# Top-k attention with two mixtures on one core: the first three weight requests of the first mixture placed behind the stores of conversion chunks 28, 30 and 31

## The chip, the cores and the metric

The kernel runs on 1 core of one Trainium2 chip. The metric is device time in microseconds, the median of several executions. TensorE is PE in the profile, VectorE DVE, ScalarE ACT, GpSimd POOL and SyncE SP.

## The reference, cut to what matters

```python
scores = q @ k.T / 8                      # 4 batches x 8 heads, 576 x 576, head size 64
scores = where(scores >= 32nd largest of the row, scores, -1e9)
x = softmax(scores) @ v                   # 2304 tokens x 512
h = x @ w_in                              # first mixture: 512 -> 2048
x = (max(h, 0) + alpha * min(h, 0)) @ w_out
# second mixture: tokens with x @ w_skip > 0 go to the best of 8 experts (512 -> 1024 -> 512)
out = x + gate * (relu(x @ w1[e]) @ w2[e])   # the other tokens keep x
```

## The kernel before, in words

Matrix products of the two mixtures are made exact enough by splitting each float32 operand into a rounded high part and the rest, and adding three products. For the first mixture the weights are split once, at the start, and the split copies are kept in device memory.

**Conversion.** `w_in` and `w_out` are cut into 32 chunks of 512 KB (`convs`). `conv_load` (lines 255 to 262) brings a raw chunk in through SP, into one half of a tile named `wr` (`cvtile`, lines 246 to 253). `convert` (lines 267 to 305) then makes three passes on ACT that read the raw chunk (lines 277, 279, 281), one on DVE (line 285), a rounding copy and a subtraction on POOL (lines 291 and 112), and a store through SP (lines 297 and 300) to `win` or `wout`. DVE's step, POOL's step and the store are put off by four slots each (`CV`, line 52), so a chunk passes through the engines while the next ones follow.

**Attention** runs in steps of 14 slots. Each slot issues what a hand-written table (`STEP`) puts there, for five units in different stages, and `slot` (line 1078) adds pieces of a list `todo` and whatever is due in the list `late`. The 32 conversions ride along in the first steps.

**The first mixture** of the first two blocks of rows starts when their attention columns are done (`queue_moe`, line 1175). Its pieces (`moe1`) multiply with `wr` tiles of 1 MB, read back from `win` and `wout` in a fixed order (`stream`). `fetch(j)` (line 569) asks for the j-th of them through POOL's queue (`wload`, line 549; the request itself is at line 551), if the chunks in it are converted and it wasn't asked for yet. There are three `wr` buffers, which conversion and mixture share: a request is held back until the buffer's last user is done. Later requests come from `need` (line 581), which asks for the weight in use, the next one and the one after that. The first three come from `store` of the last chunk:

```python
            if i == len(convs) - 1:
                late.extend((6 + j, lambda j=j: fetch(j)) for j in range(3))
```

They are issued six, seven and eight slots after chunk 31's store has been issued.

Every engine works through its own instructions in the order in which they were issued. What stands around the change is, on POOL: the last splits of `cv` tiles (chunks 29 to 31), the splits of the attention's output (`x` from `xf`, line 112) and the requests. On PE: transposes of the softmax (line 502), then the mixture's first products (`pm` from `x` and `wr`, line 604). On DVE: the attention's selection (lines 432 to 472), and the mixture's step `rn` (line 621), which needs ACT's `rn` (lines 614 and 615), which needs `pm`.

Of the kernel before, what the change touches and what calls it, by code (L numbers as in the profile page):

```python
# [62 lines left out]
def kernel(  # L63
# [46 lines left out]
    def sub(o, a, b):  # L110

        i = nc.gpsimd.tensor_tensor(o, a, b, op=OP.subtract)  # L112
        if gate[0] is not None:
            tc.add_manual_dep(i.ins, gate[0].ins.name, mybir.DependencyInfo(
                mybir.DependencyClass.Sync, mybir.DependencyReason.DATA), reason="the port is free then")
            gate[0] = None
# [120 lines left out]
    todo, late, convq, rowq = [], [], [], []  # L237
# [8 lines left out]
    def cvtile(i):  # L246

        if i:
            return moe.tile([128, 1024], F32, name="cv", tag="g", bufs=8)
        if not ring:  # L250
            t = moe.tile([128, 16, 128], F32R, name="wr", tag="wr", bufs=3).rearrange("p a c -> p (a c)").bitcast(F32)
            ring.extend(t[:, h * 1024:(h + 1) * 1024] for h in range(2))
        return ring.pop(0)

    def conv_load(kind, f):
        raw = cvtile(0).bitcast(I32).rearrange("p (d f t) -> p d f t", d=4, t=2)
        if kind == 0:
            nc.sync.dma_start(
                raw.rearrange("p d f t -> p d (f t)"),
                win32[:, f * 256:(f + 1) * 256].rearrange("(d p) f -> p d f", p=128))  # L260
        else:
            nc.sync.dma_start(raw.rearrange("p d f t -> p (d f t)"), wout32[f * 128:(f + 1) * 128, :])
        raws[kind, f] = raw

    convs = [(kd, f) for kd in range(2) for f in range(KF)]

    def convert(i):

        kind, f = convs[i]
        raw = raws.pop((kind, f))  # L270
        r2 = raw.rearrange("p d f t -> p (d f) t")
        hi, lo = r2[:, :, 1], r2[:, :, 0]
        hif = hi.bitcast(F32)
        w = cvtile(1).rearrange("p (a c) -> p a c", a=2)


        nc.scalar.activation(w[:, 0], hif, AF.Copy, scale=2.0 ** -112)
        t2 = w[:, 1].bitcast(U16).rearrange("p (c k) -> p c k", k=2)
        nc.scalar.activation(t2[:, :, 1].bitcast(mybir.dt.float16), hif, AF.Copy, scale=2.0 ** -60)
        top = raw.rearrange("p d f t -> p (d f t)").bitcast(U16).rearrange("p (c k) -> p c k", k=4)[:, :, 1]  # L280
        nc.scalar.activation(t2[:, :, 0], top, AF.Copy, scale=2.0 ** -13, bias=2.0 ** -14 - 0.5)

        def bits():
            t = w[:, 1].bitcast(I32)
            nc.vector.scalar_tensor_tensor(t, w[:, 0].bitcast(I32), 3, t, op0=OP.logical_shift_left,
                                           op1=OP.bitwise_or)
            if i + AHEAD < len(convs):
                conv_load(*convs[i + AHEAD])

        def split():  # L290
            nc.gpsimd.tensor_copy(w[:, 0].bitcast(F32R), w[:, 1])
            sub(w[:, 1].bitcast(F32R), w[:, 1], w[:, 0])

        def store():
            converted.add(i)
            if kind == 0:
                nc.sync.dma_start(win_s[f // 2][:, f % 2], w)
            else:
                for a in range(2):
                    nc.sync.dma_start(wout_s[f // 8][:, :, f % 8, a, :].rearrange("d p c -> p d c"),  # L300
                                      w[:, a].rearrange("p (d c) -> p d c", d=KD))
            if i == len(convs) - 1:
                late.extend((6 + j, lambda j=j: fetch(j)) for j in range(3))

        return none * (CV - 1) + [bits] + none * (CV - 1) + [split] + none * CV + [store]

# [242 lines left out]
    def wload(src):  # L549
        t = moe.tile([128, 16, 128], F32R, name="wr", tag="wr", bufs=3)  # L550
        nc.gpsimd.dma_start(t, src)
        return t
# [16 lines left out]
    def fetch(j):  # L569
        if j < len(stream) and j not in wr and stream[j][1] in converted:  # L570
            wr[j] = wload(stream[j][0])
# [904 lines left out]
```

## Time and profile before

| | us |
|---|---|
| median of 3 runs | 1110.81 (1108.39 to 1111.5) |
| the profiled execution | 1104.66 |
| its span, first to last instruction | 1102.9 |
| PE busy | 971.4 (88%) |
| DVE busy | 930.8 (84%) |
| ACT busy | 737.9 (67%) |
| POOL busy | 526.4 (48%) |

The span lies 1.8 us below the profiled execution's own time, and that execution is 6.2 us below the median of the runs. The conversion fills the first 145 us of the span. Busy shares are averages over stages; the rows further down come from the stretch of 30 us in which conversion ends and the mixture begins.

### The profile page before, as it was taken

What the parts mean: (1) busy time and instruction counts of PE and PEld (TensorE: products, weight loads), DVE (VectorE), ACT (ScalarE), POOL (GpSimd) and SP (SyncE); (2) the same over time, 40 slices, a digit from 0 to 9 for tenths busy, and PEclk for the clock granted to TensorE, in tenths of its full rate; (3) what the DMA queues carried; (4) which work ended last, traced back from release to release, by engine and by line L of the source; (5) the groups of instructions that cost most, each with busy time, mean ns of one, the idle gap of its engine ahead of it and who ended that gap; (6) DMA issues with size and microseconds to landing.
All of it is one profiled execution on the core that took longest, in us unless ns stands there. A gap on an engine that the chain in (4) does not pass through costs nothing.

```text
span 1102.9 us, 22357 instructions
## 1 busy us (share of the span) xinstructions
PE 971.4 (88%) x7270; PEld 854.3 (77%) x7270; DVE 930.8 (84%) x2943; ACT 737.9 (67%) x1932; POOL 526.4 (48%) x860
## 2 busy tenths in 40 slices
PE   4566469999999999899999999999999889898994
PEld 2444358888999888899888988998789778687883
DVE  6999969999998999899979989998993323798971
ACT  7978858667865785687568666856772433596860
POOL 5877746434653553366346425733552441326220
PEclk9997769999999999999989999999999998899997
DMA  8979876665675667656566676674556985799950
GB/s 246 323 233 291 252 227 203 222 217 175 214 229 179 206 209 245 205 196 218 192 196 197 215 239 218 200 227 165 181 192 241 368 308 206 276 362 397 344 197 8
DMA packets 154286, 254.17 MB, mean 230 GB/s; under 512 B 78062, under 2 KB 110830, under 8 KB 137776
## 3 DMA queue, kind: packets, MB, share of 16 engines
q0 software_dynamic: 20928, 138.73, 36.3%
q1 hardware_dynamic: 132032, 113.62, 32.9%
q8 instruction: 60, 0.98, 0.4%
q14 instruction: 66, 0.54, 0.1%
q10 hardware_dynamic: 1200, 0.30, 0.1%
HBM read 224.20 MB, written 29.71 MB: 230 GB/s over the span
## 4 chain that ended last, share of the span: by engine, by line
PE 49%; DVE 30%; DMA 8%; ACT 5%; issue 4%; POOL 3%; SPq 1%; POOLq 0%; DVEq 0%; ACTq 0%
PE pm L653 15%; PE pm L604 10%; DVE v L441 5%; DVE F L432 4%; PE px L536 4%; DVE Ex L472 4%; DVE m L432 4%; PE ps L411 4%; PE px L1029 4%; DVE F L444 4%; PE pm L1011 4%; PE pt L502 3%; DVE rn L621 3%; DMA wr<-wout 2%; DMA wr<-win 2%
## 5 line engine op out<-in xcount | busy, mean ns | idle before, releaser
L604 PE MATMUL pm<-x,wr 128*128 128x256 f32 (+1 forms) x1536 | 250.9, 311 | 16.7 <-DMA wr<-win 13.9
L653 PE MATMUL pm<-g,wr 128*128 128x256 f32 (+1 forms) x1536 | 241.4, 305 | 5.7 <-DMA wr<-wout 5.7
L604 PEld LDWEIGHTS pm<-x,wr 128*128 128x128 f32 x1536 | 217.5, 195 | 26.2 <-DMA wr<-win 9.0
L653 PEld LDWEIGHTS pm<-g,wr 128*128 128x128 f32 x1536 | 211.2, 190 | 14.4 <-issue 7.1
L441 DVE MAX8 v<-F 128x8 f32<-128x72 f32 (+2 forms) x576 | 213.1, 405 | 1.0
L416 ACT ACTIVATE sb<-ps 128x288 f32<-128x288 f32 x288 | 105.1, 413 | 95.2 <-PE ps L411 61.8
L112 POOL TENSOR_TENSOR g<-rn,g 128x256 fp32r<-128x256 f32 (+1 forms) x128 | 110.7, 874 | 71.2 <-ACT g L635 27.9
L411 PE MATMUL ps<-kT,qT 64*128 64x288 f32 x768 | 102.8, 357 | 28.5 <-ACT sb L416 15.8
L444 DVE MATCH_REPLACE8 F<-v,F 128x72 f32<-128x72 f32 (+1 forms) x432 | 122.9, 290 | 0.0
L472 DVE SCALAR_TENSOR_TENSOR Ex<-sb,v,Ex 128x577 f32<-128x577 f32 x144 | 121.3, 870 | 0.0
L411 PEld LDWEIGHTS ps<-kT,qT 64*128 64x128 f32 x768 | 66.7, 206 | 56.7 <-ACT sb L416 20.0
L621 DVE SCALAR_TENSOR_TENSOR rn<-rn,nalpha 128x256 f32<-128x256 f32 (+1 forms) x128 | 78.8, 616 | 36.4 <-ACT rn L615 34.8
L464 ACT ACTIVATE Ex<-sb,st 128x576 f32<-128x576 f32 x144 | 105.2, 780 | 0.3
L112 POOL TENSOR_TENSOR x<-xf,x 128x128 fp32r<-128x128 f32 (+1 forms) x80 | 41.3, 516 | 127.0 <-ACT x L545 121.5
L502 PE MATMUL pt<-ident,Ex 128*128 128x128 f32 x576 | 90.8, 294 | 0.0
L536 PE MATMUL px<-PT,vt 128*64 128x128 f32 (+1 forms) x1280 | 88.5, 285 | 0.0
L514 ACT ACTIVATE PT<-pt 128x512 f32<-128x512 f32 x144 | 86.4, 601 | 2.9 <-PE pt L502 2.7
L614 ACT ACTIVATE rn<-pm 128x256 f32<-128x256 f32 (+1 forms) x128 | 52.7, 412 | 52.0 <-PE pm L604 49.7
L502 PEld LDWEIGHTS pt<-ident,Ex 128*128 128x128 f32 x576 | 69.5, 149 | 10.9 <-issue 7.5
L536 PEld LDWEIGHTS px<-PT,vt 128*64 128x64 f32 x1280 | 69.5, 146 | 9.7 <-issue 1.8
L432 DVE TENSOR_TENSOR F<-m 128x144 f32<-128x144 f32 (+2 forms) x240 | 71.2, 348 | 0.0
L635 ACT ACTIVATE g<-rn 128x256 fp32r<-128x256 f32 (+1 forms) x128 | 56.4, 448 | 20.2 <-DVE rn L621 20.1
(431 smaller groups left out, 1908.8 us busy)
## 6 DMA issues: line engine op xcount, KB each, us to landing
wr<-win POOLq DMA_DIRECT2D x64, 1024.0 KB, 5.3
wr<-wout POOLq DMA_DIRECT2D x64, 1024.0 KB, 5.2
wraw<-in_moe_w_dram SPq DMA_DIRECT2D x88, 512.0 KB, 6.0
wr<-in_moe_w_in_dram SPq DMA_DIRECT2D x16, 512.0 KB, 5.4
vt<-in_v_dram SPq DMA_DIRECT2D x32, 256.0 KB, 4.0
win<-cv SPq DMA_DIRECT2D x16, 512.0 KB, 4.6
wr<-in_moe_w_out_dram SPq DMA_DIRECT2D x16, 512.0 KB, 5.0
wout<-cv SPq DMA_DIRECT2D x32, 256.0 KB, 3.3
```

The lines of the kernel that those rows point to most:

```text
L112: i = nc.gpsimd.tensor_tensor(o, a, b, op=OP.subtract)
L411: nc.tensor.matmul(self.ps[h, j][:, 0:HALF], lhsT=hd["q"][gp, a, u * 128:(u + 1) * 128], rhs=hd["k"][gp, b_, c0:c0 + HALF], **se)
L432: gate[0] = nc.vector.tensor_tensor(o[:, n_], a[:, n_, 0:w], a[:, n_, w:2 * w], op=op)
L441: nc.vector.max(v8[:, h, r, :], F[:, h, 0:w])
L444: nc.vector.match_replace(out=F[:, h, 0:w], in_to_replace=v8[:, h, r, :], in_values=F[:, h, 0:w], imm_value=NEG)
L464: nc.scalar.activation(self.Ex[:, h, :], self.sb[:, h, :], AF.Exp, bias=self.st[:, 0, h:h + 1], scale=0.125)
L472: nc.vector.scalar_tensor_tensor(self.Exp[:, cs], self.sbp[:, cs], v8[:, h, 3, 7:8], self.Exp[:, cs], op0=OP.is_ge, op1=OP.mult, accum_out ...
L502: nc.tensor.transpose(pt[:, c * 128:(c + 1) * 128], P[:, c0:c0 + 128], ident)
L536: nc.tensor.matmul(x[h * 64:(h + 1) * 64, 0:n], lhsT=hd["vt"][:, h, c, :], rhs=rhs, start=False, stop=(c == SF - 1))
L604: nc.tensor.matmul(hp[:, 0:n], lhsT=w[:, (f % 2) * 8 + a * 4 + d, :], rhs=x[:, d, c0:c1], start=(i == 0), stop=(i == 3 * KD - 1))
L621: nc.vector.scalar_tensor_tensor(rn[:, 0, 0:n], rn[:, 1, 0:n], nalpha[:, f:f + 1], rn[:, 0, 0:n], op0=OP.mult, op1=OP.add)
L653: nc.tensor.matmul(op_[:, 0:n], lhsT=w[:, 2 * f + a, :], rhs=g[(hf + ch) * 8 + f, sg][:, gg, 0:n], start=(i == 0), stop=(i == ni - 1))
```

## The change

The three requests leave the list of pieces that are put off, and are issued at once: the first right behind the store of chunk 28, the second behind that of chunk 30, the third behind that of chunk 31.

```diff
                     nc.sync.dma_start(wout_s[f // 8][:, :, f % 8, a, :].rearrange("d p c -> p d c"),
                                       w[:, a].rearrange("p (d c) -> p d c", d=KD))
-            if i == len(convs) - 1:
-                late.extend((6 + j, lambda j=j: fetch(j)) for j in range(3))
+            if i in (28, 30, 31):
+                fetch((28, 30, 31).index(i))
```

Only POOL's instructions change places; those of PE, DVE, ACT and SP stand as before. Here is POOL, from the attention output's split behind chunk 28 to the three requests, before. `cv_1434`, `cv_1481` and `cv_1510` are chunks 29, 30 and 31, `win0`, `win1` and `win2` the first three weights of the mixture.

```order
L112 TENSOR_TENSOR x_648<-xf_1473,x_648 128x128
L291 CAST cv_1434<-cv_1434 128x512
L112 TENSOR_TENSOR cv_1434<-cv_1434 128x512
L291 CAST cv_1481<-cv_1481 128x512
L112 TENSOR_TENSOR cv_1481<-cv_1481 128x512
L476 MEMSET sb_1276 128x2
L477 MEMSET Ex_1538 128x2
L291 CAST cv_1510<-cv_1510 128x512
L112 TENSOR_TENSOR cv_1510<-cv_1510 128x512
L112 TENSOR_TENSOR x_648<-xf_1592,x_648 128x128
L551 DMA wr_1598<-win0_123 128x2048
L551 DMA wr_1600<-win1_124 128x2048
```

The third request, of `win2`, follows as the next row. With the change the first of these places, behind chunk 28, reads:

```order
L112 TENSOR_TENSOR x_648<-xf_1473,x_648 128x128
L551 DMA wr_1494<-win0_123 128x2048
L291 CAST cv_1434<-cv_1434 128x512
L112 TENSOR_TENSOR cv_1434<-cv_1434 128x512
L291 CAST cv_1481<-cv_1481 128x512
```

The first request has moved up past the splits of three chunks and one split of attention output. And the second place, behind chunk 31, reads:

```order
L291 CAST cv_1512<-cv_1512 128x512
L112 TENSOR_TENSOR cv_1512<-cv_1512 128x512
L551 DMA wr_1593<-win1_124 128x2048
L112 TENSOR_TENSOR x_648<-xf_1596,x_648 128x128
L551 DMA wr_1610<-win2_125 128x2048
L112 TENSOR_TENSOR cert_119<-v8_1288 128x8
```

The second request has moved up past the last split of attention output, and the third stands where it stood. The waits of the three requests are the same as before: the landing of the raw chunks that last filled their buffers, chunks 26 and 27 for the first, 28 and 29 for the second, 30 and 31 for the third.

## Rows read from the trace of the kernel before

**Rows 1.** The chain that ended last: share of the span by engine.

```profile
PE 49%; DVE 30%; DMA 8%; ACT 5%; issue 4%; POOL 3%; SPq 1%; POOLq 0%; DVEq 0%; ACTq 0%
```

**Rows 2.** Windows: busy us of PE, PEld, DVE, ACT, POOL; PEclk, DMA share, GB/s.

```profile
143.85:149.10 5.25, 0.00 (x0) 0.00 (x0) 5.25 (x18) 0.68 (x2) 3.96 (x7) 0.50 1.00 256
149.10:152.39 3.29, 0.00 (x1) 0.01 (x1) 0.20 (x3) 0.00 (x0) 0.00 (x0) 0.50 1.02 351
152.39:156.55 4.16, 4.16 (x24) 4.04 (x26) 0.00 (x0) 1.13 (x5) 0.00 (x0) 0.66 1.05 414
156.55:163.49 6.94, 6.94 (x68) 6.31 (x68) 5.39 (x19) 6.43 (x19) 4.15 (x7) 1.00 0.31 71
```

**Rows 3.** Waits, 143 to 164 us: total us, times, longest.

```profile
ACT PT L519 <- PE pt L505: 10.1, 2, 10.0
...
DVE rn L621 <- ACT rn L615: 8.8, 2, 7.2
PE pm L604 <- DMA wr<-win: 8.6, 1, 8.6
```

**Rows 4.** Timeline of PE: start, duration, what, [idle before it <- releaser].

```profile
141.84 1.97 PE L502 MATMUL pt<-ident,Ex 128*128 128x128 f32 x8
152.39 1.65 PE L604 MATMUL pm<-x,wr 128*128 128x256 f32 x6 [8.58 <-DMA wr<-win]
...
156.41 1.09 PE L536 MATMUL px<-PT,vt 128*64 128x128 f32 x16
...
160.66 0.96 PE L604 MATMUL pm<-x,wr 128*128 128x256 f32 x6
```

**Rows 5.** Timeline of POOL, chunk 28's end to the three requests.

```profile
134.51 0.47 POOL L112 TENSOR_TENSOR x<-xf,x 128x128 fp32r<-128x128 f32 x1
...
138.17 1.14 POOL L291 CAST cv<-cv 128x512 fp32r<-128x512 f32 x1 [1.29 <-DVE cv L285]
...
143.16 1.27 POOL L112 TENSOR_TENSOR cv<-cv 128x512 fp32r<-128x512 f32 x1
144.39 1.00 POOL L112 TENSOR_TENSOR x<-xf,x 128x128 fp32r<-128x128 f32 x1
145.34 1.85 POOL L551 DMA_DIRECT2D wr<-win  x3
```

**Rows 6.** Timeline of SP: the last load of a raw chunk (chunk 31).

```profile
125.54 0.67 SPq L262 DMA_DIRECT2D wr<-in_moe_w_out_dram  x1
```

**Rows 7.** Tile wr, issue to landing: first request alone; second and third; fourth and fifth.

```profile
DMA to landing us min/median/max: 7.0/7.0/7.0
...
DMA to landing us min/median/max: 8.8/9.8/10.8
...
DMA to landing us min/median/max: 5.1/5.1/5.2
```

**Rows 8.** Timeline of DVE around the stall.

```profile
149.09 0.21 DVE L444 MATCH_REPLACE8 F<-v,F 128x72 f32<-128x72 f32 x1
156.55 0.48 DVE L621 SCALAR_TENSOR_TENSOR rn<-rn,nalpha 128x256 f32<-128x256 f32 x1 [7.25 <-ACT rn L615]
...
157.63 0.28 DVE L543 TENSOR_TENSOR xf<-px,R 128x128 f32<-128x128 f32 x1
...
163.49 0.49 DVE L621 SCALAR_TENSOR_TENSOR rn<-rn,nalpha 128x256 f32<-128x256 f32 x1 [1.55 <-ACT rn L615]
```

**Rows 9.** Windows as in rows 2: the clock while PE works, before and after the stall.

```profile
94.00:114.00 20.00, 12.99 (x69) 9.30 (x69) 19.95 (x57) 16.36 (x41) 16.86 (x24) 0.50 0.97 276
114.00:116.00 2.00, 1.34 (x14) 1.10 (x12) 2.00 (x4) 2.00 (x6) 1.92 (x3) 0.93 1.04 344
...
152.00:155.00 3.00, 2.61 (x12) 2.62 (x13) 0.00 (x0) 0.45 (x2) 0.00 (x0) 0.50 1.03 410
155.00:155.50 0.50, 0.50 (x5) 0.50 (x5) 0.00 (x0) 0.00 (x0) 0.00 (x0) 0.74 1.22 492
```

**Rows 10.** Timeline of PE, the start of its work before the clock rose at 114 us.

```profile
110.18 1.54 PE L343 MATMUL pt<-ident,nat 128*128 128x128 f32 x6 [0.85 <-ACT PT L514]
```

## The prediction

> **What bounds the kernel now.** Over the whole span the chain that ended last lies on PE for 49% and on DVE for 30% [rows 1], so no engine's share alone tells what this edit is worth. It is read from the stretch in which conversion ends and the first mixture begins, in this order: windows, then waits, then the timelines of the engines in them.
>
> The windows show a hole. From 143.85 to 149.10 us PE does nothing, while DVE still works through attention; from 149.10 to 152.39 no engine works, apart from DVE's last 0.20 us; behind that PE is busy without a break [rows 2]. The waits name one cause: PE waits 8.6 us for the first weight of the mixture; ACT waits 10.0 us for PE, and DVE 7.2 us for ACT [rows 3]. These are one wait seen three times, so they must not be added. PE's timeline gives its edges: the last transposes end at 141.84 + 1.97 = 143.81, the first products start at 152.39 [rows 4].
>
> POOL's timeline shows why the weight is late. The three requests are issued from 145.34 on, right behind the attention output's split of 144.39 [rows 5], and the first needs 7.0 us to land [rows 7]: 145.3 + 7.0 = 152.3, when PE starts. Here a request in a queue is the bound, not an engine.
>
> **The change, part by part.** No instruction is added or removed; three requests stay three, 1.85 us of POOL together [rows 5]. Only two of them move, on POOL.
>
> *The first request* moves from behind chunk 31 to behind the split that ends at 134.51 + 0.47 = 134.98 [rows 5], 10.4 us earlier. What could hold it there is the load of chunks 26 and 27, whose buffer it takes. The last raw load of all, chunk 31, was issued at 125.54 [rows 6], and even with the slowest landing shown, 10.8 us [rows 7], it is in by 137; chunk 27's was issued before it. So I count no wait on POOL. Landing: between 5.1 and 10.8 us [rows 7], so at 140.1 to 145.8. I take 7.0, what this very request took, as it again shares the DMA engines with loads and stores: 142.0, 1.8 us before PE is free. Then the wait of 8.58 us [rows 4] is gone; at the slow end it is 152.39 - 145.8 = 6.6 us.
>
> *What is behind it on POOL.* The splits of chunk 29 start some 0.6 us later, but POOL then idles 1.29 us for DVE ahead of chunk 30's copy [rows 5], which hides it; without that cover the price would be 0.6 us of the stores. *The second request* now stands ahead of the split of 144.39, which then ends at 145.9 instead of 145.3. PE needs that split only in the second half of its first sum, after six products of 1.65 us in all [rows 4] and some transposes, so not before 145.5: a cost between 0 and 0.4 us, and I take 0, since the transposes fill most of it.
>
> *What is late next: the clock.* PE restarts at the lower of its two levels, 1.2 GHz: the granted clock is 0.50 from 152 to 155, and 0.74 in the half microsecond after it [rows 9], so that PE works about 2.9 us at half rate. With the change PE goes on at 143.81, again at 0.50. How long it stays there no row shows. At the near end it is 2.9 us again, and costs nothing. The other rise in reach came around 114.1, 3.9 us behind the work that began at 110.18 [rows 9, 10]; at the far end stands the stretch from 94 to 114, where PE worked 13.0 us and the clock never rose [rows 9]. Each extra microsecond at half rate costs half a microsecond. I take 5 us, nearer to the two rises since PE's work is dense: (5 - 2.9) / 2 = 1.1 us. In my own range I allow 8 us, or 2.5.
>
> *DVE.* It works until 149.09 + 0.21 = 149.30 on what is ready, and then wants `rn`, which came 156.55 - 152.39 = 4.16 us behind PE's restart [rows 4, 8]. From 143.81 this is 148.0, or 149.1 with the slower clock: DVE goes straight on and gains its idle 7.25 us. At 163.49 it waited 1.55 us more for the same chain PE to ACT [rows 8]; a part of that wait remains, and sets DVE's lead to PE's, 8.6 - 1.1 = 7.5 us. The attention product `px` is done at 156.41 + 1.09 = 157.50 and used by DVE at 157.63 [rows 4, 8]; moved by 7.5 and by 7.25 they are 150.0 and 150.4, so that no new wait stands there. *The third request* stays in its place, 0.6 us after its neighbour's old one, and its weight is used last of the three: no cost.
>
> **Sum:** -8.6 for the wait, +1.1 for the clock, 0 for POOL: **-7.5 us**. Everything behind is relative to these engines, since no later work starts at a fixed time; so I carry it to the end. Against its own time the profiled execution goes from 1104.66 to 1097.2. The median of the runs shown is 6.2 us higher; the same step on it gives 1110.81 - 7.5 = **1103.3 us**.
>
> **The rivals.**
>
> *The second request takes the first one's place* (9%). It moves up 1.6 us, to 143.16 + 1.27 = 144.4 [rows 5]; its products, at 160.66 before [rows 4], come at 153.2. If it takes 7.0 us like the first of the burst before, it lands at 151.4; with 8.8 at 153.2, just in time; with 10.8 [rows 7] at 155.2, and PE waits 2.0: -5.5 us, 1105.3. For it: the three requests issued while DVE was busy all through [rows 2] took 7.0 to 10.8 us, the next two 5.1 and 5.2 [rows 7]. Against: these three also queued behind each other. The Trainium skill (SBUF — State Buffer, section on SBUF's two separate sides) says that a DVE operation holding the port shared with GpSimd keeps GpSimd from writing the descriptors of its requests. By that rule the second request stays slow whatever has left the queue ahead of it; the rows fit that as well as a shared queue, and don't decide.
>
> *The clock stays down until about 155*, as it did in the run before (9%): PE then works 11.5 us at 0.50 instead of 2.9, which takes back 4.3: -4.3 us, 1106.5. For it: the stretch from 94 to 114 [rows 9], and the eight transposes right ahead of 143.81 [rows 4] that left the clock at 0.50. The Trainium skill (TensorE: Matmul & The Clock Gate, part 4 on the PE-mode transpose) states that transposes don't count as busy for the gate in the way that products do. By that rule the transposes between the mixture's first products would keep the clock down longer; the same mixture of work raised it in 3 us before [rows 9], which speaks against.
>
> *Slower* (3%), by the same mechanism carried on: the gain is used up when PE has worked 17 us more at half rate than before, so if the clock stays down past 164. Held down until 175 it would cost 28.3 / 2 - 8.6 = +5.5 us, 1116.3. Against: behind the restart PE is busy 4.16 of 4.16 and 6.94 of 6.94 us [rows 2], denser than from 94 to 114.
>
> *No change* (8%), 1110.8: the request moves but does not leave earlier, held on POOL by something that the names of its waits don't show, or DVE's and PE's later waits give the time back. Against: the raw loads are in by then, and from 149.10 to 152.39 no engine has work at all, so that at least these 3.3 us can't be cover for anything.
>
> **How the numbers follow.** The forecast has 71%; its own range is 6.0 (8 us at half rate) to 8.6 us of gain, with 1.5 us either way for the median, half of what three runs spread: 1100.7 to 1106.3. To hold 8 in 10, the upper end is moved to take in both milder rivals, up to a gain of no more than the empty 3.3 us: 1107.5. A measurement can tell about 0.3%, 3.3 us, from no change. Forecast and the first two rivals are faster by more; a few hundredths of them may be lost in the runs' spread. That gives 0.85 faster, 0.11 the same, 0.04 slower.
>
> **What would show it.** Right: POOL's first request near 135.0, landing before 143.8; the first products of the mixture within 1 us of 143.8, with no wait for `win` ahead; DVE's 7.25 us idle gone; PE's later work 7 to 8 us earlier, at 300 us as at 900. Wrong: a request that leaves near 145 still; a wait of PE for the second weight near 153; a clock of 0.50 past 152 (then the gain is 4 to 6 us); or a lead at 160 us that is gone later.

## The result, and the profile after

| | before | with the change |
|---|---|---|
| median of 20 runs, us | 1108.04 (1103.77 to 1115.5) | 1098.58 (1092.58 to 1105.31) |
| ratio | | 0.9907 (0.9890 to 0.9924) |
| the profiled execution, us | 1104.66 | 1097.02 |
| its span, us | 1102.9 | 1095.2 |

The change is 9.5 us faster by the medians and 7.6 us by the two profiled executions. The time lies below the predicted range, which ended at 1100.7. Two things moved: the median of the kernel before came down from 1110.81 of 3 runs to 1108.04 of 20, and the gain is larger than the 7.5 us forecast. The ratio is worked out from the fast runs and is not the quotient of the two medians, which is 0.9915.

The page of the changed kernel, its span, two engines and the chain that ended last; the shares that answer to them stand in the table of the kernel before and in [rows 1]:

```profile
span 1095.2 us, 22357 instructions
...
PE 970.3 (89%) x7270; PEld 853.4 (78%) x7270; DVE 931.4 (85%) x2943; ACT 737.4 (67%) x1932; POOL 526.3 (48%) x860
...
PE 46%; DVE 36%; DMA 6%; ACT 4%; issue 4%; POOL 3%; SPq 0%; POOLq 0%; DVEq 0%; ACTq 0%
```

Busy times are what they were within 1.1 us; what went is idle time, and the chain's share on DMA.

Windows of the changed kernel, the same four stretches as [rows 2]:

```profile
143.85:149.10 5.25, 4.56 (x44) 4.07 (x43) 5.22 (x11) 3.07 (x10) 4.36 (x7) 0.91 1.00 269
149.10:152.39 3.29, 3.29 (x31) 2.83 (x29) 3.29 (x18) 2.83 (x9) 1.42 (x4) 1.00 1.05 386
152.39:156.55 4.16, 4.09 (x36) 3.91 (x35) 4.16 (x13) 3.54 (x14) 1.73 (x3) 1.00 1.17 335
156.55:163.49 6.94, 6.94 (x67) 6.65 (x66) 6.94 (x28) 5.86 (x19) 5.47 (x11) 1.00 0.82 267
```

The hole is filled: where no engine worked from 149.10 to 152.39, PE and DVE are now busy throughout. DVE, the third busy time of a row, now has work in all of these 19.6 us but 0.03. PE has small gaps, so here DVE sets the pace.

PE's timeline, changed kernel (answers to [rows 4]):

```profile
141.81 1.97 PE L502 MATMUL pt<-ident,Ex 128*128 128x128 f32 x8
143.43 1.55 PE L604 MATMUL pm<-x,wr 128*128 128x256 f32 x6
...
146.22 0.86 PE L604 MATMUL pm<-x,wr 128*128 128x256 f32 x5 [0.69 <-POOL x L112]
```

POOL's timeline, changed kernel (answers to [rows 5]):

```profile
134.88 0.74 POOL L551 DMA_DIRECT2D wr<-win  x1
135.61 0.64 POOL L291 CAST cv<-cv 128x512 fp32r<-128x512 f32 x1
136.33 1.27 POOL L112 TENSOR_TENSOR cv<-cv 128x512 fp32r<-128x512 f32 x1
...
145.11 0.57 POOL L551 DMA_DIRECT2D wr<-win  x1
145.70 0.47 POOL L112 TENSOR_TENSOR x<-xf,x 128x128 fp32r<-128x128 f32 x1
```

DVE's timeline, changed kernel (answers to [rows 8]); the first row is a step of the attention:

```profile
136.41 1.81 DVE L472 SCALAR_TENSOR_TENSOR Ex<-sb,v,Ex 128x577 f32<-128x577 f32 x1
...
150.58 1.05 DVE L621 SCALAR_TENSOR_TENSOR rn<-rn,nalpha 128x256 f32<-128x256 f32 x1
...
156.45 0.48 DVE L621 SCALAR_TENSOR_TENSOR rn<-rn,nalpha 128x256 f32<-128x256 f32 x1
```

The request leaves at 134.88, the mixture's first products start at 143.43 without a wait, 8.96 us earlier, and DVE's waits of 7.25 and 1.55 us for `rn` are gone. But DVE's step of line 621 that stood at 163.49 [rows 8] comes only 7.04 us earlier, at 156.45. The first row shows part of why: it took 1.81 us. In the kernel before, the same step, its next turn, and POOL's subtraction of chunk 29 were:

```profile
136.45 1.05 DVE L472 SCALAR_TENSOR_TENSOR Ex<-sb,v,Ex 128x577 f32<-128x577 f32 x1
...
138.03 0.81 DVE L472 SCALAR_TENSOR_TENSOR Ex<-sb,v,Ex 128x577 f32<-128x577 f32 x1
...
135.61 1.27 POOL L112 TENSOR_TENSOR cv<-cv 128x512 fp32r<-128x512 f32 x1
```

Before, the subtraction ended at 136.88 and the step 0.62 us behind it, at 137.50. With the change the subtraction, pushed back by the request, runs from 136.33 to 137.60, and the step again ends 0.62 us behind it, at 138.22. So the two met before as well, at a cost of 0.24 us against the 0.81 of the next turn; with the change the cost is 1.00, 0.76 us more. At that next turn DVE's step started first, and POOL took longer: the copy of 138.17 [rows 5], begun 0.14 us behind it, took 1.14 us, the copy of 135.61 further up 0.64.

### The profile page after: what moved, and what is told of

It is laid out like the page before. It is cut to its first block, busy times and chain, and to the rows that moved or that the text cites. A ratio compares the mean times of both kernels' runs of the same rounds, so it can differ in the third digit from the quotient of the medians.

```text
span 1095.2 us, 22357 instructions
## 1 busy us (share of the span) xinstructions
PE 970.3 (89%) x7270; PEld 853.4 (78%) x7270; DVE 931.4 (85%) x2943; ACT 737.4 (67%) x1932; POOL 526.3 (48%) x860
## 4 chain that ended last, share of the span: by engine, by line
PE 46%; DVE 36%; DMA 6%; ACT 4%; issue 4%; POOL 3%; SPq 0%; POOLq 0%; DVEq 0%; ACTq 0%
PE pm L653 15%; PE pm L604 8%; DVE v L441 7%; DVE F L432 5%; DVE Ex L472 5%; DVE F L444 4%; DVE m L432 4%; PE px L1029 4%; PE px L536 4%; PE ps L411 4%; PE pm L1011 4%; PE pt L502 3%; DVE rn L621 3%; DMA wr<-wout 3%; DVE cv L285 2%
## 5 line engine op out<-in xcount | busy, mean ns | idle before, releaser
L635 ACT ACTIVATE g<-rn 128x256 fp32r<-128x256 f32 (+1 forms) x128 | 56.1, 447 | 19.6 <-DVE rn L621 19.4
```

## The experiments

To compare profiles I take the time from PE's product at line 532 near 124.7 us, before the order changes, to the first product with `w_out` near 200 us, behind the stall. These are its ends, before and then changed, in PE's timeline:

```profile
124.80 0.79 PE L532 MATMUL px<-PT,vbd 128*128 128x128 f32 x2
...
198.91 0.97 PE L653 MATMUL pm<-g,wr 128*128 128x256 f32 x6
```

```profile
124.77 0.78 PE L532 MATMUL px<-PT,vbd 128*128 128x128 f32 x2
...
191.60 0.97 PE L653 MATMUL pm<-g,wr 128*128 128x256 f32 x6
```

So this stretch is 74.1 us before and 66.8 us with the change, 7.3 apart. For all kernels, in the order in which they are told (ratio to the kernel before, with its interval):

| kernel | ratio | stretch, us | half clock behind the restart, us |
|---|---|---|---|
| before | | 74.1 | 2.9 |
| no delay, old order | 0.9993 (0.9975 to 1.0012) | 75.2 | 5.1 |
| before, second profile | | 75.4 | 6.1 |
| before, third profile | | 75.5 | 4.5 |
| changed | 0.9907 (0.9890 to 0.9924) | 66.8 | 1.3 |
| changed, again | 0.9930 (0.9905 to 0.9955) | 66.6 | 2.3 |
| changed, third | 0.9912 (0.9883 to 0.9941) | 66.9 | 0 |
| first request alone | 0.9956 (0.9929 to 0.9984) | 67.6 | 2.9 |
| first behind chunk 29 | 0.9928 (0.9901 to 0.9954) | 66.2 | 2.1 |
| behind 28, 29, 30 | 0.9902 (0.9868 to 0.9937) | 66.8 | 0 |
| two behind chunk 29 | 0.9896 (0.9871 to 0.9921) | 66.1 | 1.8 |
| the same, again | 0.9891 (0.9850 to 0.9932) | 66.1 | 0 |
| middle dose | 0.9995 (0.9975 to 1.0016) | 73.3 | 4.0 |
| products in the wait | 0.9992 (0.9970 to 1.0013) | 73.7 | see below |

The last column is the time from the mixture's first products to the rise of the granted clock, worked out from windows of 1 us (a value of 0.87 is 0.26 us at 0.50 and the rest at 1.00); 0 means that it stood at 1.00 already.

**The delay, or the place in the queue.** All three requests at once behind chunk 31, which gives POOL the old order:

```diff
-            if i in (28, 30, 31):
-                fetch((28, 30, 31).index(i))
+            if i == len(convs) - 1:
+                for j in range(3):
+                    fetch(j)
```

> All three requests issued at once behind chunk 31's store, without the six to eight slots of delay. On POOL they then stand where they stood before, behind the last split of attention output. Theory A (the gain is the first request's place in POOL's queue, and through it PE's wait): no change, ratio 0.997 to 1.003, first products of the mixture at 152.4 +- 0.5, and PE's wait of 8.6 us is there again. Theory B (it is the delay by slots that cost time, whatever the place in the queue): most of the gain, ratio 0.990 to 0.994. This run also tells how far two measurements of one order differ.

Ratio 0.9993: no change, first products at 152.20. PE's wait is there again, 10.0 us instead of 8.6, since PE was done sooner, at 142.2. Theory B falls: the delay by slots costs nothing that these runs can tell, and it is the place in POOL's queue that counts. The run was also a second look at the old order, and differs from the first. Windows of this kernel, 1 us each:

```profile
143.00:144.00 1.00, 0.00 (x0) 0.00 (x0) 0.96 (x3) 0.24 (x2) 1.00 (x1) 0.84 1.03 289
...
152.00:153.00 1.00, 0.80 (x3) 0.80 (x4) 0.00 (x0) 0.00 (x0) 0.00 (x0) 0.50 1.02 410
...
157.00:158.00 1.00, 1.00 (x16) 0.81 (x16) 0.87 (x7) 1.00 (x3) 0.69 (x1) 0.83 0.15 34
```

Here the clock was full until 143.7, fell in the wait, and rose only at 157.3, 5.1 us behind the restart instead of 2.9.

**The change again**, twice.

> The changed kernel once more. The profiled pair showed a lead of 7.3 us from 175 to 360 us and 7.7 us at the end, the medians 9.5 us. Theory A1 (the stall is worth 7 to 8 us and the rest is spread between executions): ratio 0.9925 to 0.9940, and the first product with w_out starts 7 to 8 us before the 198.9 us of the kernel before. Theory A2 (the stall itself is longer in most executions than in the profiled one, because the first weight lands later than 7.0 us): ratio near 0.990, a lead again of 7 to 8 us against the profiled kernel before, but a kernel before whose first weight lands later when profiled again.

> The changed kernel a third time, for what is open in the size: two comparisons gave 0.9907 (0.9890 to 0.9924) and 0.9930 (0.9905 to 0.9955); the profiles of the two orders stand 7.3 to 8.9 us apart at 200 us. If the stall with its clock is all of it, 0.992 to 0.9935; if there is a second gain beyond it, 0.990 to 0.991 again.

Ratios 0.9930 and 0.9912, stretches 66.6 and 66.9 us. The three profiles of the change agree within 0.3 us. The mark of theory A2, the time from the request to the first products, is 7.05, 7.18, 6.88 and 7.63 us in the four profiles of the old order (152.39 - 145.34, 152.20 - 145.02, 152.93 - 146.05, 152.80 - 145.17): the landing differs by 0.6 us at most from the one that the prediction used, too little for the 2 us that the medians gained beyond it.

**The first request alone.**

```diff
-            if i in (28, 30, 31):
-                fetch((28, 30, 31).index(i))
+            if i == 28:
+                fetch(0)
+            if i == len(convs) - 1:
+                late.extend((6 + j, lambda j=j: fetch(j)) for j in range(1, 3))
```

> Only the first request moves, the second and third stay where they were before. Theory A: the whole gain, ratio within 0.002 of the changed kernel's, first products near 143.5; without the second request ahead of it the last split of attention output ends 0.6 us earlier and PE's wait of 0.7 us for it shrinks. Rival (the second request's earlier place is part of the gain): PE waits for the second weight near 152 and 1 to 2 us of the gain are lost.

First products at 143.37 as expected, but now the second weight is waited for. PE's waits from 140 to 160 us:

```profile
PE pm L606 <- DMA wr<-win: 1.9, 1, 1.9
```

The stretch is 67.6 us, 0.8 more than with the change. So the rival has a point: moving the second request up is worth most of a microsecond. The ratio lost more than that, 0.9956 against 0.9930 of the changed kernel beside it, more than the 0.002 expected; the medians of the two, over that of the kernel before, are 0.9937 and 0.9924, and the intervals overlap. Runs of this spread don't say how much was lost.

**The first request one chunk later.**

```diff
-            if i in (28, 30, 31):
-                fetch((28, 30, 31).index(i))
+            if i in (29, 30, 31):
+                fetch((29, 30, 31).index(i))
```

> The first request behind chunk 29's store instead of chunk 28's: on POOL behind the splits of chunk 29, so issued near 136.9 instead of 134.9. With 7.0 us to land it is in at 143.9, when PE is free at 143.8. Theory A: the same gain within 0.5 us, as 1.8 us of slack are used up and no more. Rival (the landing takes longer while raw loads and stores run): first products at 145 to 147, 1 to 3 us of the gain lost.

The mixture starts at 143.22 and PE waits for no weight: the slack was there. The stretch is even 0.6 us shorter than with the change, 66.2. DVE's step of line 472 takes what it took in the kernel before, since POOL's subtraction stands where it stood:

```profile
136.21 1.04 DVE L472 SCALAR_TENSOR_TENSOR Ex<-sb,v,Ex 128x577 f32<-128x577 f32 x1
```

**All three a step earlier; two behind chunk 29.**

```diff
-            if i in (28, 30, 31):
-                fetch((28, 30, 31).index(i))
+            if i in (28, 29, 30):
+                fetch((28, 29, 30).index(i))
```

> Requests behind the stores of chunks 28, 29 and 30: the second now leaves near 137.7 instead of 145.0, the third near 145 instead of 146. If the second weight is what PE waits for next (0.9 us in one profile of the changed kernel, 1.9 us with only the first request moved, none in the other two), that wait is gone in every profile, and the lead at 200 us is 0 to 1 us above the changed kernel's 7.3 to 7.6. Against it: the split of chunk 29 still collides with DVE's step of 136.4 (1.81 us in place of 1.05), which costs DVE 0.7 us. Ratio 0.990 to 0.993.

```diff
-            if i in (28, 30, 31):
-                fetch((28, 30, 31).index(i))
+            if i == 29:
+                fetch(0)
+                fetch(1)
+            elif i == 30:
+                fetch(2)
```

> First and second request together behind chunk 29's store, the third behind chunk 30's. No request stands ahead of chunk 29's splits, so DVE's step of 136.3 should take 1.05 us again and not 1.81; the two requests fall into POOL's idle 1.3 us ahead of chunk 30's copy, of which they take 1.3. The first lands at 143.5 to 145, the second before 150. Lead at 200 us: 8 to 8.5 us, as with the first request behind chunk 29 (8.1), and never a wait for the second weight. Ratio 0.990 to 0.993. Rival: the first shares the DMA engines with the second and lands at 146 or later: lead 6 to 7.

> The variant without the collision on DVE a second time, beside the changed kernel on the same chip. Its profile showed a lead of 8.0 us at 200 us, counted from 130 us, against 7.3 and 7.4 of the changed kernel. If that holds in time, its ratio is 0.0005 to 0.001 below the changed kernel's, which is less than these runs can tell; a difference of 0.002 or more in either direction would speak of something else.

With all three earlier PE never waits for a weight and runs at the full clock from the mixture's start on, and the stretch is 66.8 us all the same: DVE sets it, and its step of line 472 takes 1.81 us here too. With two behind chunk 29, where that step takes 1.04 and 1.05 us, both profiles give 66.1 us, 0.7 less than the changed kernel's mean. That is the price of the longer collision. In time, 0.9896 and 0.9891 stand beside 0.9907 to 0.9930: lower, but the intervals overlap, so that it beats the change is shown in the stretch and not in the runs. In one of its two profiles PE does wait 0.3 us for a weight, at the start.

**The old order, profiled again.**

> The kernel before once more, for its profile. The two profiles of its order so far differ by 0.8 us at 165 us: the clock rose at 155.1 in one and at 157.2 in the other. Theory C: in this one too, PE's start near 152.3 stands in the range of 152.0 to 152.6, and where the clock rises later the whole of the mixture is later by half the difference. Rival: the landing of the first weight differs by more than 0.5 us between profiles and explains the 0.8 us.

> The kernel before, a further profile. Theory C: behind PE's restart near 152.4 the clock stands at half for 2.9 us or more. Rival: it rises within 2.8 us, as in the changed kernel's profiles, and the difference between the orders seen so far was chance.

The stretch is 75.4 and 75.5 us; the half-rate work behind the restart 6.1 and 4.5 us. In the second profile PE starts at 152.93, outside the 152.0 to 152.6 expected, but there the whole stretch begins 0.7 us late, at 125.53. The windows of the third profile end like those of the kernel without the delay:

```profile
152.00:153.00 1.00, 0.20 (x1) 0.20 (x2) 0.00 (x0) 0.00 (x0) 0.00 (x0) 0.50 1.03 410
...
157.00:158.00 1.00, 1.00 (x13) 0.88 (x13) 0.69 (x4) 1.00 (x5) 0.09 (x1) 0.83 0.31 70
```

DVE's waits for PE and ACT, 130 to 175 us, in that profile and then in the second:

```profile
DVE rn L621 <- ACT rn L615: 9.8, 2, 8.2
DVE xf L543 <- PE px L536: 0.3, 1, 0.3
```

```profile
DVE rn L621 <- ACT rn L615: 9.0, 2, 7.4
DVE xf L543 <- PE px L536: 1.0, 1, 1.0
```

They sum to 10.1 and 10.0 us, and to 9.9 in the kernel without the delay (9.4 and 0.5), against 8.8 in the profile that the prediction was made from [rows 3]. The first profile was the mildest of four. In the second the first weight even landed soonest, so there the clock is the whole of it; in the third the landing has a share of 0.6 us.

**Products in the wait.** 48 products that need no weight, ahead of the mixture's first sum, in the kernel before:

```diff
                 hps[0] = mtile()
             hp = hps[0]
+            if base == 0 and wi == 0 and first:
+                for _ in range(48):
+                    nc.tensor.matmul(hp[:, 0:n], lhsT=xh[:, 0, 0:128], rhs=xh[:, 1, c0:c1], start=True, stop=True)
```

> The kernel before, with 48 products of 256 columns put ahead of the mixture's first sum, into the same bank, which the first real product then starts anew. They need no weight, so they run in the 8.6 us in which PE waits, and the output is the same. They take 0.11 us each at the full clock and 0.22 at half, so 5 to 10 us. Theory C (a part of the stall's cost is that PE restarts at half rate: 2.9 us of it in one profile of this order, 5.0 in the other, against 1.2 to 2.3 us with the request moved): the first weight lands as before near 152.3, the products then run at the full clock, and the kernel gains 1.5 to 2.5 us at 200 us, ratio 0.9975 to 0.9985. Rival (the clock falls again by 152, or DVE sets the pace there anyway): no gain, ratio 0.999 to 1.001.

PE's timeline of this kernel:

```profile
143.41 6.61 PE L603 MATMUL pm<-x 128*128 128x256 f32 x48
153.10 0.98 PE L607 MATMUL pm<-x,wr 128*128 128x256 f32 x6 [3.07 <-DMA wr<-win]
```

The clock rose at 144.8 and stayed up, and the first six products took 0.98 us instead of 1.65. The weight landed 0.7 us later than in the first profile, and the stretch is still the shortest of the old order with its requests unmoved, 73.7 us against 74.1 to 75.5. Against the first profile that is 0.4 us gained in spite of 0.7 lost, so the clock is worth around 1 us here. In the runs it can't be seen (0.9970 to 1.0013), and the expected ratio lies inside that: inconclusive in time.

**A middle dose.**

```diff
-            if i in (28, 30, 31):
-                fetch((28, 30, 31).index(i))
+            if i == 29:
+                late.append((2, lambda: fetch(0)))
+            elif i in (30, 31):
+                fetch(i - 29)
```

> A middle dose: the first request behind the splits of chunk 30, so issued near 142.5, between 134.9 of the change and 145.3 before. With 7 us to land, the mixture starts at 149.5, and PE waits 5.7 us. Theory A (when the mixture starts is set by this request's place on POOL alone): first products at 149 to 151, a wait of PE of 5 to 7 us, lead at 200 us of 2 to 4 us. Theory C on the clock: since PE idles 5 us or more ahead of it, its clock stands at half for 2.9 us or more behind the restart, as in the three profiles with the old order (2.9, 5.0 and 6.1 us), not 0 to 2.8 us as in the profiles with the request moved. Ratio 0.995 to 0.999.

POOL issues the request at 142.04; PE's timeline and the landing:

```profile
150.76 1.65 PE L606 MATMUL pm<-x,wr 128*128 128x256 f32 x6 [7.29 <-DMA wr<-win]
```

```profile
DMA to landing us min/median/max: 8.8/8.8/8.8
```

The start is where theory A put it, but on a landing of 8.8 us, not 7. PE waited 7.3 us, more than the 5 to 7 expected, and the clock stood at half for 4.0 us, as theory C had it. 3.3 us of earlier request gave 1.6 us of earlier start. The stretch is shorter by 0.8 us than in the first profile of the old order and by 1.7 than the mean of its four, less than the 2 to 4 expected, and the runs can't tell it from nothing. DVE's idle time in the stretch is 7.5 us, against 10.0 on average in the old order, but its busy time is 65.9, against 65.0: a part of what the wait gives back goes into longer steps.

## Why the prediction was wrong in size, and right in kind

**What held.** The request in POOL's queue was the bound; the raw loads didn't hold it; it left at 134.88 (forecast 135.0) and landed before PE was free; products started at 143.4 (143.8); the waits of PE, ACT and DVE went together. The table shows that the place on POOL does it; for the delay in slots it shows no cost. And DVE, which sets the pace, kept 0.3 us of idle time in each of the three profiles of the change, so the second request and the split behind it, for which PE waited up to 1.3 us each, cost next to nothing there: the text had put both at 0.

**What failed first: the clock's term,** "(5 - 2.9) / 2 = 1.1 us". I let PE run 5 us at half rate behind its new start, and the kernel before 2.9. It is the other way round. (One of the rises it went by, read at 114.1, was at 114.3 by the 0.93 of [rows 9].) With the first request ahead of chunk 30, in eight profiles of five orders, the clock was up 0 to 2.9 us after the start, 1.3 on average; with PE waiting, in five profiles, it took 2.9 to 6.1 us, 4.5 on average. With the change PE has worked almost without a break since 136.5 when the mixture starts. On PE the term is (1.3 - 4.5) / 2 = -1.6 us instead of +1.1. The second rival let the transposes hold the clock down until about 155, by what the Trainium skill says of them (TensorE: Matmul & The Clock Gate, part 4 on the PE-mode transpose); the clock was up by 146.3 in every profile with the first request ahead of chunk 30, with those transposes around and among the products. That speaks against what the rival made of the rule, and not against the rule.

**What failed second: DVE's lead was set equal to PE's.** PE got more than forecast and DVE, which sets the pace from then on, couldn't use all of it. DVE's lead in the profiled pair is its idle time, 7.25 + 1.55 = 8.8, less some 1.5 us by which its own work grew: 0.76 in the step at 136.4, 0.57 in the first `rn` (1.05 instead of 0.48), 0.54 in three steps of line 432 just ahead of it (1.42 instead of 0.88), and some 0.3 back in smaller changes both ways. That is the 7.3 us measured. For the request ahead of chunk 29's splits the text had nothing, or 0.6 us of the stores without POOL's 1.29 us of idle time; POOL did have the idle time, but its shifted subtraction met more of DVE's step, and DVE paid. The variants that leave the subtraction in its place get 0.6 to 0.7 us back. The rule of the Trainium skill that DVE and GpSimd exclude each other from a shared port for a whole operation (SBUF — State Buffer, section on SBUF's two separate sides) fits in the main: POOL's subtraction ran from 136.33 to 137.60, and DVE's step, begun at 136.41, ended at 138.22. In seven profiles of four orders the step ended 0.61 to 0.63 us behind the subtraction, so it moves with it. A step that had done nothing until then would have needed its 0.81 us; some 0.2 us of it was done by then.

So 7.5 agreed with 7.3 by luck: two errors cancelled, against a profile that was no average. Over the four profiles of the old order the stretch is 75.1 us, over three of the change 66.8: **8.3 us**. In the sum's own terms: -9.7 for DVE's waits (mean of 8.8, 9.9, 10.0 and 10.1), +1.4 for the growth of its own work (66.45 us busy in the stretch instead of 65.02), a term that the forecast didn't have.

**And the base.** 1103.3 was counted down from a median of three runs. From the 20-run median the same forecast would have been 1100.5, and its range 1097.9 to 1104.7 would have held 1098.58. I gave that median 1.5 us either way; it was 2.8 off. Of the 4.7 us between 1103.3 and 1098.58 this is 2.8, and the gain beyond 7.5 the other 2.0, of which the stretch accounts for 0.8.

**What stays open.** The three comparisons of the change, weighted by the inverse squares of their intervals' half-widths (0.0017, 0.0025, 0.0029), give 0.9914 with 0.0013 either way: 8.1 to 10.9 us of 1106. The stall's 8.3 lies near the lower end of that. The medians of the three comparisons differ by 9.5, 8.3 and 8.7 us. Whether 1 us more comes from elsewhere, these runs don't tell: behind the stretch the four profiles of the old order last 901.6 to 904.4 us, the three of the change 900.7 to 903.6. Executions of the old order spread over 12 us, while the stretch with the stall differs by 1.4 us between its profiles, so most of that spread seems to lie elsewhere.

**The rivals.** The second request did become a wait in two of the three profiles of the change, 0.9 and 1.2 us, as the first rival had it, but with 1.9 us alone in the variant where it wasn't moved, and PE had that to spare, as DVE's 0.3 us of idle time shows. It took 6.7 and 8.0 us to land in two profiles although the first had long left the queue; that fits a DVE that holds off POOL's descriptors, by the rule of the Trainium skill cited there, and as well the stores of the last chunks beside it. No run separates the two, and no row shows whether DVE's steps of that time held the port that the descriptors need. The clock staying down to 155 and the slower case didn't occur. No change is excluded by all three intervals.

## What to carry to other kernels

Where all engines idle together, find the one request they wait for and how early it could have been issued; place it so that it lands before its user is free, since a request 3.3 us earlier, of the 10.5 of the change, bought 1.7 us of the stretch and nothing that the runs could tell. Before sizing such a stall by one profile, ask which parts of it differ between executions (here the clock behind the wait and the landing), and which engine will be the bound once it is gone: its lead, with what the moved work now collides with, is the gain. And a median of three runs is a base with an error of its own, to be added to the range.

## What the runs showed of the hardware that was not expected

A wait costs more than its length: with PE idle 7 to 10.5 us, the clock stayed at 0.50 for 2.9 to 6.1 us of work behind it, and in two profiles it had been at 1.00 until 143.7, so PE lost a level that it had. Where the wait was gone, the clock was up at the start or within 2.9 us; in the three profiles in which it was at 1.00 by 143, that level was kept. Here is the window of the changed kernel's third profile that answers to the first one of the kernel without the delay:

```profile
143.00:144.00 1.00, 0.39 (x3) 0.39 (x4) 0.96 (x5) 0.75 (x3) 0.92 (x5) 1.00 1.11 320
```

A first weight of 1 MB took 6.4 to 8.8 us to land among the last chunks' loads and stores, against 5.1 later [rows 7]; the slowest, requested at 142.04, left after the earlier ones and before the later, so its place alone doesn't set it. And 0.7 us of queue delay on POOL, for which POOL had idle time, came out as 0.76 us on DVE, whose step kept ending 0.62 us behind POOL's subtraction.
